# Gated spectral filter and token MLP: the order of the last two additions, and the last token block in two column halves

## The chip, the cores and the metric

The kernel runs on one core of a Trainium2 chip. The metric is the device time of one execution in microseconds; a profiled execution also gives a trace of every engine. TensorE (PE) multiplies matrices into PSUM, ScalarE (ACT) and VectorE (DVE) read PSUM and write SBUF, GpSimd (POOL) works on SBUF, and SyncE (SP) issues all transfers.

## The reference

Two branches work on the same input `x` of 2048 tokens by 512 channels, in bf16, and are blended per token by a sigmoid gate. Branch A is a two-dimensional FFT, a product with complex weights, and the inverse FFT. Branch B is a layernorm followed by an MLP over the token axis (2048 to 1792 to 2048).

```python
def _A_ref(x, w_r, w_i):
    X = rfft2(x.astype(float32), axes=(-2, -1))
    X = X * (w_r + 1j * w_i)
    return irfft2(X, s=(S, D)).astype(bfloat16)

def _B_ref(x, w1, b1, w2, b2):
    h = _layernorm(x, axis=-1)
    u = gelu(einsum("bsd,sf->bdf", h, w1) + b1)
    y = einsum("bdf,fs->bds", u, w2) + b2
    return y.transpose(0, 2, 1)

g = sigmoid((x * gate_w).sum(-1, keepdims=True))
return g * a + (1 - g) * b
```

## The kernel before

Tokens lie on the 128 partitions in 16 blocks: block `r` holds one token for each partition and all 512 channels, a tile of 128x512. `x` and `hn` in SBUF hold the 16 blocks of the input and of its layernorm. `tb` is another name for `x`: the result of block `r` is written over the input block `r`, which nobody reads any more by then. In the same way `z3` is another name for `hn`.

Branch B runs in two products. The first multiplies `hn` by the weights `w1` and goes through GELU on ScalarE (line 478) into `gl`, 14 tiles of 128x512. The second product (line 749) makes block `r` out of 14 matmuls, one for each tile of `gl`, that accumulate in one PSUM bank. Its weights for block `r`, 448 KB, are loaded ahead into a slot of the SBUF tiles `w1a` or `w1b` (line 746), whose first contents are used up by then; blocks 14 and 15 use slots 8 and 9 of `w1a` again.

Branch A is a chain of short matrix products with evictions, two round trips through DRAM and an elementwise product between them. It ends in a transform of each block: one matmul with the 128x128 matrix `t1i` and the block `z3[r]` (line 759).

The two branches meet at the end. The gate `g` becomes three tables with one column per block: `omg` is 1 - g, `omb` is (1 - g) times the bias b2, and `gs` is g times the scale of the inverse FFT; POOL makes them out of a tanh on ScalarE (lines 736 to 740). For each block:

- ScalarE evicts the second product with its scale and bias: `tb[r] = omg * product + omb`, bf16 (line 752, named `ye`).
- VectorE adds the transform from PSUM: `tb[r] = gs * transform + tb[r]` (line 762, named `fin`).
- SP sends `tb[r]` to DRAM, 128 KB (line 765, named `out`).

PSUM has eight banks. Four are handed out in pairs (the pool `pair`: the transforms of two blocks share one), and four singly (the pool `fb`: one for each second product).

The order on every engine is written out by a planner, the class `Plan` (lines 39 to 165). Each operation is added with an engine, an estimated cost in ns, a priority (a lower one goes first), and keys that it reads and writes. The planner repeats one step: of all operations whose inputs and buffers are known, it takes the one that can start earliest by the estimates, and among equals the one with the lower priority, and then the one added first. That fixes each engine's order; the engines then run in this order and wait for each other by semaphores. So the place in the program text decides only between equals. Priorities that matter here: `T1i` (transform) 60 + r, second product 300 + r, load of its weights 62 + 3.05 r, outputs 200.

Of the kernel before, what the change touches and what calls it, by code (L numbers as in the profile page):

```python
# [8 lines left out]
ActF = mybir.ActivationFunctionType  # L9
# [6 lines left out]
D = 512  # L16
NR = 16
NG = 16
NQ = 4
NPAIR = 2  # L20
F = 1792
NFT = 14
# [16 lines left out]
class Plan:  # L39
# [13 lines left out]
    def add(self, eng, cost, emit, prio, r=(), w=(), name="", nbytes=0, h=(), acq=(), t0=0.0):  # L53
        op = Op()
        op.eng, op.cost, op.emit, op.prio, op.name, op.bytes = eng, cost, emit, prio, name, nbytes
        op.deps, op.succ, op.ready, op.end, op.start = set(), [], t0, None, None
        op.seq = len(self.ops)
        op.acq = tuple(acq)
        op.holds = tuple(set(h) | set(acq))
        for x in op.holds:  # L60
            x.left += 1
            if x in op.acq:
                x.by = op
            else:
                op.deps.add(x.by)
        for k in r:
            if k in self.last_write:
                op.deps.add(self.last_write[k])
            self.readers.setdefault(k, []).append(op)
        for k in w:  # L70
            if k in self.last_write:
                op.deps.add(self.last_write[k])
            for o in self.readers.get(k, ()):
                op.deps.add(o)
            self.last_write[k] = op
            self.readers[k] = []
        op.deps.discard(op)
        self.ops.append(op)
        return op
# [89 lines left out]
def kernel(  # L169
# [17 lines left out]
    add = pl.add  # L187
    V, A, G, T, Q = nc.vector, nc.scalar, nc.gpsimd, nc.tensor, nc.sync
# [4 lines left out]
    x = sb([P, NR, D], "x")  # L193
    hn = sb([P, NR, D], "hn")
    gl = sb([P, NFT, D], "gl")
# [32 lines left out]
    omg = sb([P, NR], "omg", F32)  # L228
    gs = sb([P, NR], "gs", F32)
    omb = sb([P, NR], "omb", F32)  # L230
# [3 lines left out]
    ps = psp.tile([P, 8, 512], F32, name="ps")  # L234
# [3 lines left out]
    tb = x  # L238
# [8 lines left out]
    for b in range(0, NR, 2):  # L247
        k = b // 2
# [63 lines left out]
    mul, plus, band, shr = Alu.mult, Alu.add, Alu.bitwise_and, Alu.arith_shift_right  # L312
# [12 lines left out]
    for k, (n, sh, m) in enumerate(BITS):  # L325
        add("DVE", 75, lambda k=k, sh=sh, m=m: V.tensor_scalar(ci[:, k:k + 1], pcol, sh, m, op0=shr, op1=band), -94,
            r=["pcol"], w=[("ci", k)], name=n)
    add("DVE", 90, lambda: V.tensor_copy(cf[:, 0:len(BITS)], ci[:]), -93, r=[("ci", k) for k in range(len(BITS))],
        w=[("c", n) for n in col], name="cf")
# [63 lines left out]
    for j in range(4):  # L393
        for cc in range(2):
            add("ACT", 600, lambda j=j, cc=cc: A.activation(t2v[:, :, cc, :, j], svv[:, cc], ActF.Copy,  # L395
                                                            scale=f(f"d{j}")), 1.5, r=["sv", ("c", f"d{j}")] + TMPK, w=["t2"])
# [30 lines left out]
    for k, (o, s, key) in enumerate(((768.0, ecol[:, 0:1], "ecol"), (768.0, ecol[:, 1:2], "ecol"),  # L427
# [11 lines left out]
        r=["rrow", ("c", "ck")] + TMPK, w=["rg"])  # L439
# [9 lines left out]
        r=["sv2"] + [("c", f"d{j}") for j in range(4)] + TMPK, w=["t2i"], name="exp", t0=28000.0)  # L449
# [14 lines left out]
    for b in range(NR):  # L464
        add("DVE", 605, lambda b=b: V.bn_stats(out=stats[:, b, :], in_=x[:, b, :]), b, r=[("x", b)],  # L465
            w=[("stats", b)], name="bn")
        add("DVE", 90, lambda b=b: V.bn_aggr(out=mv[:, b, :], in_=stats[:, b, :]), b - 0.5, r=[("stats", b)],  # L467
            w=[("mv", b)], name="aggr")
        add("DVE", 62, lambda b=b: V.tensor_single_scalar(mv[:, b, 1:2], mv[:, b, 1:2], 1e-5, op=plus), b - 0.6,
            w=[("mv", b)], name="eps")  # L470
# [3 lines left out]
                                                    op0=Alu.subtract, op1=mul), b - 10,  # L474
            r=[("x", b), ("mv", b), ("rstd", b)], w=[("hn", b)], name="hn")
# [10 lines left out]
    for b in range(NR):  # L486
        for ft in range(FT1):
# [3 lines left out]
                stop=(b == NR - 1)), 100 + b if b < 13 else 113 + 0.1 * ft,  # L491
                r=[("w1a", b), ("hn", b)] + [("over", b, j) for j in range(b * 768 // 2048, ((b + 1) * 768 - 1) // 2048 + 1)],
                w=[("acc", ft)],
                name="p1", h=[hold], acq=[hold] if b == 0 and first else [])
# [12 lines left out]
    for k in range(NFT - FT1):  # L507
        ft = FT1 + k
        w, wk, wl = wslot(k)
        load(w, w1bh[k].rearrange("a r f -> a (r f)"), 26 + 3.45 * k, wl, 524288)  # L510
        wv = w.rearrange("p (r f) -> p r f", f=P)
        hb = Hold("fb")
# [8 lines left out]
    for r2 in range(8):  # L521
        hs = Hold("sth")
        for k in range(2):
            r = 2 * r2 + k
            add("PE", 216, lambda r=r, k=k: T.matmul(ps[:, k], lhsT=t1[:], rhs=x[:, r, :], start=True,  # L525
                                                     stop=True), 10 + r, r=["t1", ("x", r)],
                w=[("psT", k)], name="T1", h=[ht], acq=[ht] if r == 0 else [])
            add("ACT", 480, lambda hs=hs, k=k: A.copy(st4[:, hs.idx, k], ps[:, k]), 0,  # L528
                r=[("psT", k)], w=[("st1", r2)], name="T1e", h=[ht], acq=[hs] if k == 0 else [])
        add("SP", 440, lambda r2=r2, hs=hs: Q.dma_start(out=scr1[2 * r2:2 * r2 + 2].rearrange("r p d -> p r d"),  # L530
                                                        in_=st4[:, hs.idx]), 5.5, r=[("st1", r2)],
            w=[("scr1", r2)], nbytes=262144, name="w1", h=[hs])
    s1v = scr1[:].rearrange("r (c g) d -> (r c) g d", g=NG)
    zh = [Hold("zz", q) for q in range(NQ)]
    for q in range(NQ):
        add("SP", 440, lambda q=q: Q.dma_start(out=z2[:, 4 * q:4 * q + 4], in_=s1v[:, 4 * q:4 * q + 4]), 6 + 0.1 * q,
            r=[("scr1", k) for k in range(8)], w=[("z2", q)], nbytes=524288, name="r1", h=[zh[q]], acq=[zh[q]])

    def pslot(hold, k):
        return ps[:, 2 * hold.idx + k]  # L540
# [7 lines left out]
    for q in range(NQ):  # L548
# [3 lines left out]
        for h in range(2):  # L552
            hp = Hold("pair")
            for k in range(2):
                g = 4 * q + 2 * h + k
                for s in range(4):
                    add("PE", 56, lambda g=g, s=s, k=k, hp=hp: T.matmul(  # L557
                        pslot(hp, k)[:, s * P:(s + 1) * P], lhsT=z2[:, g, s * P:(s + 1) * P],
                        rhs=t2[:, g].rearrange("p k c l i -> p (k c l i)"), start=True, stop=True),
                        20 + q, r=["t2", ("z2", q)], w=[kq("pT2", h, k, s)], name="T2", h=[hp, zh[q]],  # L560
                        acq=[hp] if k == 0 and s == 0 else [])
# [3 lines left out]
                r=[kq("pT2", h, k, s) for k in range(2) for s in range(4)], w=[kq("t2o", h)], name="T2e",  # L565
                h=[hp, ht2], acq=[ht2] if h == 0 else [])
# [6 lines left out]
        def fold2(V_op, sl, ht2=ht2, hpm=hpm, hfo=hfo):  # L573
# [4 lines left out]
            acq=[hpm])  # L578
# [3 lines left out]
            name="f2", h=[hpm], acq=[hfo])  # L582
        add("DVE", 605, lambda f=fold2: f(V.tensor_sub, slice(1, 3)), 50, r=pmk, w=[kq("fo", 1), kq("fo", 2)],
            name="f2", h=[hpm, hfo])
        for t in range(2):
            hp = Hold("pair")
            for e in range(2):
# [3 lines left out]
                    r=["td", kq("fo", cl)], w=[kq("pD", cl)], name="D", h=[hp, hfo], acq=[hp] if e == 0 else [])  # L591
            add("ACT", 905, lambda t=t, hp=hp, huv=huv: A.copy(uv[:, huv.idx, t], pview(hp)), 2.5,  # L592
                r=[kq("pD", 2 * t), kq("pD", 2 * t + 1)], w=[kq("uv", t)], name="De", h=[hp, huv],
                acq=[huv] if t == 0 else [])
# [15 lines left out]
        def Yv(hy=hy):  # L610
# [5 lines left out]
            h=[huv], acq=[hx])  # L616
        add("DVE", 605, lambda U=U, W_=W_, X=X: V.tensor_sub(X()[:, :, 2:0:-1], U(), W_()), pw, r=uk, w=xk, name="w",
            h=[huv, hx])
        for s in range(2):
            def wv_(m, s=s):  # L620
# [3 lines left out]
                r=xk + [("wq", q)], w=tk, name="w", h=[hx, htb], acq=[htb] if s == 0 else [])  # L624
            add("DVE", 605, lambda X=X, m=wr, wv_=wv_, ss_=ss_: V.tensor_mul(X()[:, :, ss_], X()[:, :, ss_], wv_(m)), pw,
                r=[("wq", q)], w=xk, name="w", h=[hx])
        add("DVE", 605, lambda X=X: V.tensor_sub(X()[:, :, 0:4:3], X()[:, :, 0:4:3], tbw[:, :, 1:3]), pw, r=tk, w=xk,
            name="w", h=[hx, htb])
        add("DVE", 605, lambda X=X: V.tensor_add(X()[:, :, 1:3], X()[:, :, 1:3], tbw[:, :, 0:4:3]), pw, r=tk, w=xk,
            name="w", h=[hx, htb])  # L630
        add("DVE", 605, lambda X=X, Yv=Yv: V.tensor_add(Yv()[:, 0], X()[:, :, 0:2], X()[:, :, 2:4]), pw, r=xk, w=yk,
            name="w", h=[hx], acq=[hy])
        add("DVE", 605, lambda X=X, Yv=Yv: V.tensor_sub(Yv()[:, 1], X()[:, :, 3::-3], X()[:, :, 1:3]), pw, r=xk, w=yk,
            name="w", h=[hx, hy])
        if q == 0:
# [3 lines left out]
            for k, (t, c_) in enumerate(((0, 0), (1, 1), (1, 0), (0, 1))):  # L639
                add("POOL", 400, lambda k=k, t=t, c_=c_: G.tensor_tensor(spt[:, k], sUV(t), w0[c_], op=mul), 0,  # L640
                    r=uk + [("wq", 0)], w=["spt"], h=[huv])
            add("POOL", 400, lambda: G.tensor_tensor(spc[:, 0], spt[:, 0], spt[:, 1], op=plus), 0, r=["spt"], w=["spc"])
            add("POOL", 400, lambda: G.tensor_tensor(spc[:, 1], spt[:, 2], spt[:, 3], op=Alu.subtract), 0, r=["spt"],
                w=["spc"])
            for t in range(2):
                add("DVE", 90, lambda t=t, Y=Y: V.tensor_copy(
                    Y()[:, t].rearrange("p e n (c k) -> p e n c k", c=2)[:, :, 0, :, 0], spc[:, t]), 59, r=["spc"],
                    w=yk, h=[hy])
# [3 lines left out]
                r=["lw"], w=["li"])  # L652
            ts("POOL", 250, lr[:], lr[:], 0.5, None, mul, None, 0, [], ["lr"])
            ts("POOL", 250, li[:], li[:], 0.5, None, mul, None, 0, [], ["li"])
        for t in range(2):
            add("SP", 440, lambda q=q, t=t, huv=huv: Q.dma_start(
                out=lf[16 * t:16 * t + 16, q].rearrange("p c k -> p (c k)"),
                in_=uv[0:1, huv.idx, t, 0].rearrange("o (n c) -> o n c", c=32)), 5, r=[kq("uv", t)],
                w=[kq("lf", t)], nbytes=20000, name="lane", h=[huv])
        lk = [kq("lf", 0), kq("lf", 1)]  # L660
        add("POOL", 400, lambda q=q: G.tensor_tensor(lt[:, 0], lf[:, q], lr[:, q], op=mul), 0, r=lk + ["lr"],
            w=["lt"])
# [3 lines left out]
            r=["lt"], w=[kq("lo")])  # L666
        add("POOL", 400, lambda q=q: G.tensor_tensor(lo[:, q, 1], lt[:, 0, 1], lt[:, 1, 0], op=plus), 0,
            r=["lt"], w=[kq("lo")])
        for t in range(2):
            add("SP", 440, lambda Y=Y, q=q, t=t: Q.dma_start(  # L670
                out=Y()[0:1, t, 0], in_=lo[16 * t:16 * t + 16, q].rearrange("p c k -> p (c k)")), 4,
                r=[kq("lo")] + yk, w=[kq("yl", t)], nbytes=20000, name="lane", h=[hy])
# [6 lines left out]
        for h in range(2):  # L679
            hp = Hold("pair")  # L680
            first = True
            for cl, (t, e) in ((1, (0, 1)), (3, (1, 1)), (0, (0, 0)), (2, (1, 0))):
                for k in range(2):
# [3 lines left out]
                        lhsT=Y()[:, t, e, n:n + 4].rearrange("p n c -> p (n c)"),  # L687
                        rhs=tdi[:, cl], start=True, stop=True), 40 + q,
                        r=["tdi"] + yk + ([kq("yl", t)] if e == 0 else []), w=[kq("pI", h, k, cl)],
                        name="Di", h=[hp, hy], acq=[hp] if first else [])  # L690
# [49 lines left out]
    add("POOL", 200, lambda: G.tensor_tensor(omb[:], omg[:], smf[:, 14:30], op=mul), 0, r=["omg", "smf"], w=["omb"])  # L740

    slots = [8, 9, 10, 11, 12, 13, 0, 1, 2, 3, 4, 5, 6, 7, 8, 9]
    for r in range(NR):
        w, wk, wl = wslot(slots[r])
        wv = w[:, 0:NFT * P].rearrange("p (t a) -> p t a", a=P)
        load(wv, w2h[r], 62 + 3.05 * r, wl, 458752)
        hb = Hold("fb")
        for ft in range(NFT):
            add("PE", 216, lambda ft=ft, wv=wv, hb=hb: T.matmul(  # L749
                ps[:, 2 * NPAIR + hb.idx], lhsT=wv[:, ft], rhs=gl[:, ft, :], start=(ft == 0), stop=(ft == NFT - 1)),  # L750
                300 + r, r=wk + [("gl", ft)], w=[("y", r)], name="p2", h=[hb], acq=[hb] if ft == 0 else [])
        add("ACT", 665, lambda r=r, hb=hb: A.activation(tb[:, r, :], ps[:, 2 * NPAIR + hb.idx], ActF.Identity,  # L752
                                                        bias=omb[:, r:r + 1], scale=omg[:, r:r + 1]), 2.2,
            r=[("y", r), "omb", "omg"], w=[("x", r)], name="ye", h=[hb])
    for r2 in range(NR // 2):
        hp = Hold("pair")
        for k in range(2):
            r = 2 * r2 + k
            add("PE", 216, lambda r=r, hp=hp, k=k: T.matmul(pslot(hp, k), lhsT=t1i[:], rhs=z3[:, r, :], start=True,  # L759
                                                            stop=True), 60 + r, r=["t1i", ("hn", r)],  # L760
                w=[("pL", r)], name="T1i", h=[hp], acq=[hp] if k == 0 else [])
            add("DVE", 660, lambda r=r, hp=hp, k=k: V.scalar_tensor_tensor(  # L762
                tb[:, r, :], pslot(hp, k), gs[:, r:r + 1], tb[:, r, :], op0=mul, op1=plus), 30,
                r=[("pL", r), "gs"], w=[("x", r)], name="fin", h=[hp])
            add("SP", 440, lambda r=r: Q.dma_start(out=out[r], in_=tb[:, r, :]), 200, r=[("x", r)], w=[("out", r)],
                nbytes=131072, name="out")
    pl.run()
    global _PLAN
    _PLAN = pl
# [69 lines left out]
```

## Time and profile before

| | |
|---|---|
| Median of 6 runs | 135.73 us |
| Lowest and highest of the 6 | 133.41 and 137.38 us |
| Profiled execution, its own time | 133.49 us |
| Its span, first to last instruction | 131.7 us |
| Mean granted TensorE clock | 0.994 |
| TensorE busy | 123.5 us (94%) in 648 matmuls |
| VectorE, ScalarE, POOL busy | 93.8, 71.4, 41.0 us |
| Second product: matmuls, booked length of one | 224, 379 ns |
| Last step on ScalarE (line 752), mean of one | 782 ns, 16 times |
| Last step on VectorE (line 762), mean of one | 746 ns, 16 times |
| Output of a block, issue to landing | 1.7 us (median), 16 times |

The profiled execution took 2.2 us less than the median of the other runs; the runs themselves are 4 us apart. Busy time of TensorE counts the booked length of each matmul, from its start to the end of its passage through the array; matmuls overlap, so the distance between two starts tells what one costs in a stream. "Issue to landing" of a transfer runs from the instruction on SP to the arrival of its last bytes.

### The profile page before, as it was taken

To read this page: it belongs to the slowest core of one execution; us is meant where nothing else is said; L and a number is where in the kernel's file an instruction comes from. 1 tells how busy PE (TensorE), PEld (TensorE's weight loads), DVE (VectorE), ACT (ScalarE), POOL (GpSimd) and SP (SyncE) were. 2 spreads that over 40 slices of the span, in tenths; PEclk is the share of its full clock that TensorE was granted. 3 is DMA by queue.
4 is the path that set the end of the run, shared out by engine and by line. 5 is a ranking of instruction groups with operands and counts; after the bars stand their busy time and mean duration, and the time that the engine had idled before them with its cause. 6 is when DMAs were issued, how large, how long until landed. Compare 5 with 4: busy or idle time off the path is not lost.

```text
span 131.7 us, 1982 instructions
## 1 busy us (share of the span) xinstructions
PE 123.5 (94%) x648; PEld 58.0 (44%) x648; DVE 93.8 (71%) x245; ACT 71.4 (54%) x98; POOL 41.0 (31%) x87
## 2 busy tenths in 40 slices
PE   6979999999799999999989999999999999999960
PEld 2223444443565444445445454544444444444420
DVE  7999899889799979999999998803400089322221
ACT  5378899169685784763254668539572222113320
POOL 5299964970440049997270000000000000000000
PEclk9999999999999999999999999999999999999997
DMA  4999989998989899999995327210323985411111
GB/s 119 266 331 386 339 185 388 353 373 294 346 281 348 299 335 314 291 340 329 344 380 168 135 43 260 96 69 0 159 98 130 362 285 200 163 41 40 40 40 40
DMA packets 15962, 29.67 MB, mean 225 GB/s; under 512 B 1968, under 2 KB 10320, under 8 KB 15952
## 3 DMA queue, kind: packets, MB, share of 16 engines
q1 hardware_dynamic: 15952, 29.55, 65.6%
q8 instruction: 5, 0.08, 0.2%
q14 instruction: 5, 0.04, 0.1%
HBM read 23.23 MB, written 6.29 MB: 224 GB/s over the span
## 4 chain that ended last, share of the span: by engine, by line
PE 71%; DMA 17%; ACT 5%; SPq 2%; issue 1%; DVE 1%
PE ps L749 37%; PE ps L514 16%; DMA x<-in_x_dram 5%; DMA scr_104<-st 4%; DMA z_66<-scr_104 4%; PE ps L489 4%; DMA yw<-lo 4%; PE ps L557 3%; PE ps L685 3%; PE ps L759 3%; PE ps L718 3%; PE ps L589 3%; SPq L245 2%; ACT st L528 2%; ACT t_76 L395 2%; PE ps L525 1%
## 5 line engine op out<-in xcount | busy, mean ns | idle before, releaser
L514 PE MATMUL ps<-hn,w1b 128*128 128x512 bf16 x128 | 30.7, 379 | 0.0
L762 DVE SCALAR_TENSOR_TENSOR x<-ps,gs,x 128x512 bf16<-128x512 f32 x16 | 11.1, 746 | 24.0 <-PE ps L759 12.1
L752 ACT ACTIVATE x<-ps,omb,omg 128x512 bf16<-128x512 f32 x16 | 12.5, 782 | 27.3 <-PE ps L749 27.3
L749 PE MATMUL ps<-gl,w1a 128*128 128x512 bf16 x112 | 26.6, 379 | 0.0
L749 PE MATMUL ps<-gl,w1b 128*128 128x512 bf16 x112 | 25.6, 379 | 0.0
L489 PE MATMUL ps<-hn,w1a 128*128 128x512 bf16 x96 | 22.8, 379 | 0.0
L514 PEld LDWEIGHTS <-w1b 128*128 128x128 bf16 x128 | 12.1, 98 | 12.7
L749 PEld LDWEIGHTS <-w1b 128*128 128x128 bf16 x112 | 11.0, 98 | 13.2
L749 PEld LDWEIGHTS <-w1a 128*128 128x128 bf16 x112 | 10.7, 98 | 11.4
L478 ACT ACTIVATE gl<-ps,smf 128x512 bf16<-128x512 f32 x14 | 9.1, 693 | 9.9 <-PE ps L514 9.0
L489 PEld LDWEIGHTS <-w1a 128*128 128x128 bf16 x96 | 9.4, 98 | 11.1 <-issue 0.2
L528 ACT CAST st<-ps 128x512 bf16<-128x512 f32 x16 | 9.2, 608 | 4.4 <-PE ps L525 3.4
L471 POOL TENSOR_TENSOR rstd<-mv,cst 128x1 f32<-128x1 f32 x16 | 9.9, 633 | 5.4 <-DVE mv L467 3.2
L733 DVE CUSTOM_DVE_ANT_0 junk<-x,gwb 128x512 bf16<-128x512 bf16 x16 | 11.2, 697 | 0.2
L465 DVE BATCH_NORM_STATS2 stats<-x 128x6 f32<-128x512 bf16 x16 | 10.6, 670 | 0.0
L692 ACT CAST z_66<-ps 128x1024 bf16<-128x1024 f32 x8 | 7.7, 1014 | 4.8 <-PE ps L685 4.8
L699 DVE TENSOR_TENSOR big<-z_66 128x1024 bf16<-128x1024 bf16 x8 | 5.4, 685 | 6.6 <-ACT z_66 L692 6.6
L592 ACT CAST uv<-ps 128x1024 bf16<-128x1024 f32 x8 | 7.9, 1017 | 2.4 <-DMA lf<-uv 1.9
L722 ACT CAST st<-ps 128x1024 bf16<-128x1024 f32 x8 | 7.8, 1018 | 2.5 <-PE ps L718 2.3
L562 ACT CAST big<-ps 128x1024 bf16<-128x1024 f32 x8 | 7.8, 1013 | 1.2 <-PE ps L557 1.1
L525 PE MATMUL ps<-x,t_80 128*128 128x512 bf16 x16 | 6.7, 439 | 1.3 <-DMA x<-in_x_dram 1.1
L473 DVE TENSOR_SCALAR hn<-x,mv,rstd 128x512 bf16<-128x512 bf16 x16 | 6.7, 432 | 0.6 <-POOL rstd L471 0.5
(100 smaller groups left out, 152.4 us busy)
## 6 DMA issues: line engine op xcount, KB each, us to landing
w1b<-in_w1b_dram SPq DMA_DIRECT2D x8, 512.0 KB, 5.2
w1a<-in_w_dram SPq DMA_DIRECT2D x8, 448.0 KB, 4.9
w1b<-in_w_dram SPq DMA_DIRECT2D x8, 448.0 KB, 5.0
w1a<-in_w1a_dram SPq DMA_DIRECT2D x8, 384.0 KB, 6.2
x<-in_x_dram SPq DMA_DIRECT2D x8, 256.0 KB, 5.8
scr_104<-st SPq DMA_DIRECT2D x8, 256.0 KB, 5.8
z_66<-scr_104 SPq DMA_DIRECT2D x4, 512.0 KB, 6.9
wq<-in_wf_dram SPq DMA_DIRECT2D x4, 512.0 KB, 5.0
```

What stands on the lines that cost most here:

```text
L465: add("DVE", 605, lambda b=b: V.bn_stats(out=stats[:, b, :], in_=x[:, b, :]), b, r=[("x", b)], w=[("stats", b)], name="bn")
L471: add("POOL", 530, lambda b=b: G.tensor_tensor(rstd[:, b:b + 1], mv[:, b, 1:2], cst[:, 1:2], op=Alu.pow), b - 200, r=[("mv", b), "cst"], w ...
L478: add("ACT", 572, lambda: A.activation(gl[:, ft, :], ps[:, bank()], ActF.Gelu_apprx_tanh, bias=smf[:, ft:ft + 1], scale=1.0), prio, r=r + ...
L489: add("PE", 216, lambda b=b, ft=ft, bank=bank: T.matmul(ps[:, bank()], lhsT=w1a[:, b, ft * P:(ft + 1) * P], rhs=hn[:, b, :], start=(b == 0 ...
L514: add("PE", 216, lambda b=b, wv=wv, hb=hb: T.matmul(ps[:, 2 * NPAIR + hb.idx], lhsT=wv[:, b], rhs=hn[:, b, :], start=(b == 0), stop=(b == ...
L525: add("PE", 216, lambda r=r, k=k: T.matmul(ps[:, k], lhsT=t1[:], rhs=x[:, r, :], start=True, stop=True), 10 + r, r=["t1", ("x", r)], w=[(" ...
L528: add("ACT", 480, lambda hs=hs, k=k: A.copy(st4[:, hs.idx, k], ps[:, k]), 0, r=[("psT", k)], w=[("st1", r2)], name="T1e", h=[ht], acq=[hs] ...
L592: add("ACT", 905, lambda t=t, hp=hp, huv=huv: A.copy(uv[:, huv.idx, t], pview(hp)), 2.5, r=[kq("pD", 2 * t), kq("pD", 2 * t + 1)], w=[kq(" ...
L733: add("DVE", 735, lambda b=b: V.tensor_tensor_reduce(junk[:], x[:, b, :], gwb[:], 1.0, 0.0, mul, plus, accum_out=glog[:, b:b + 1]), 61.5, ...
L749: add("PE", 216, lambda ft=ft, wv=wv, hb=hb: T.matmul(ps[:, 2 * NPAIR + hb.idx], lhsT=wv[:, ft], rhs=gl[:, ft, :], start=(ft == 0), stop=( ...
L752: add("ACT", 665, lambda r=r, hb=hb: A.activation(tb[:, r, :], ps[:, 2 * NPAIR + hb.idx], ActF.Identity, bias=omb[:, r:r + 1], scale=omg[: ...
L762: add("DVE", 660, lambda r=r, hp=hp, k=k: V.scalar_tensor_tensor(tb[:, r, :], pslot(hp, k), gs[:, r:r + 1], tb[:, r, :], op0=mul, op1=plus ...
```

## The change

For the last two blocks, 14 and 15, the two additions swap their order. ScalarE first evicts the transform with its gate and the bias: `tb[r] = gs * transform + omb` (named `ab`). VectorE then adds the second product straight from PSUM: `tb[r] = omg * product + tb[r]` (named `fin`). For blocks 0 to 13 nothing is changed.

The second product of block 15 is cut into two halves of 256 columns, each with its own PSUM bank, its own 14 matmuls, its own `fin` and its own output of 64 KB. The loop over the second product becomes a function `second(r)`; it is called for blocks 0 to 13 where the loop stood, and for 14 and 15 behind the transforms, since `fin` reads what `ab` writes. The cost given to the planner for a half is 108 instead of 216 ns for a matmul and 390 instead of 660 ns for `fin`.

```diff
     slots = [8, 9, 10, 11, 12, 13, 0, 1, 2, 3, 4, 5, 6, 7, 8, 9]
-    for r in range(NR):
+    def second(r):
         w, wk, wl = wslot(slots[r])
         wv = w[:, 0:NFT * P].rearrange("p (t a) -> p t a", a=P)
         load(wv, w2h[r], 62 + 3.05 * r, wl, 458752)
-        hb = Hold("fb")
-        for ft in range(NFT):
-            add("PE", 216, lambda ft=ft, wv=wv, hb=hb: T.matmul(
-                ps[:, 2 * NPAIR + hb.idx], lhsT=wv[:, ft], rhs=gl[:, ft, :], start=(ft == 0), stop=(ft == NFT - 1)),
-                300 + r, r=wk + [("gl", ft)], w=[("y", r)], name="p2", h=[hb], acq=[hb] if ft == 0 else [])
-        add("ACT", 665, lambda r=r, hb=hb: A.activation(tb[:, r, :], ps[:, 2 * NPAIR + hb.idx], ActF.Identity,
-                                                        bias=omb[:, r:r + 1], scale=omg[:, r:r + 1]), 2.2,
-            r=[("y", r), "omb", "omg"], w=[("x", r)], name="ye", h=[hb])
+        for c in range(2 if r == NR - 1 else 1):
+            cs = slice(256 * c, 256 * c + 256) if r == NR - 1 else slice(0, D)
+            hb = Hold("fb")
+            for ft in range(NFT):
+                add("PE", 216 if r < NR - 1 else 108, lambda ft=ft, wv=wv, hb=hb, cs=cs: T.matmul(
+                    ps[:, 2 * NPAIR + hb.idx, cs], lhsT=wv[:, ft], rhs=gl[:, ft, cs], start=(ft == 0),
+                    stop=(ft == NFT - 1)), 300 + r, r=wk + [("gl", ft)], w=[("y", r, c)], name="p2", h=[hb],
+                    acq=[hb] if ft == 0 else [])
+            if r < NR - 2:
+                add("ACT", 665, lambda r=r, hb=hb: A.activation(tb[:, r, :], ps[:, 2 * NPAIR + hb.idx], ActF.Identity,
+                                                                bias=omb[:, r:r + 1], scale=omg[:, r:r + 1]), 2.2,
+                    r=[("y", r, c), "omb", "omg"], w=[("x", r)], name="ye", h=[hb])
+            else:
+                add("DVE", 660 if r < NR - 1 else 390, lambda r=r, hb=hb, cs=cs: V.scalar_tensor_tensor(
+                    tb[:, r, cs], ps[:, 2 * NPAIR + hb.idx, cs], omg[:, r:r + 1], tb[:, r, cs], op0=mul, op1=plus), 30,
+                    r=[("y", r, c), "omg", ("ab", r)], w=[("x", r, c)], name="fin", h=[hb])
+                add("SP", 440, lambda r=r, cs=cs: Q.dma_start(out=out[r][:, cs], in_=tb[:, r, cs]), 200, r=[("x", r, c)],
+                    w=[("out", r, c)], nbytes=131072 if r < NR - 1 else 65536, name="out")
+
+    for r in range(NR - 2):
+        second(r)
     for r2 in range(NR // 2):
         hp = Hold("pair")
         for k in range(2):
...
+            if r >= NR - 2:
+                add("ACT", 665, lambda r=r, hp=hp, k=k: A.activation(tb[:, r, :], pslot(hp, k), ActF.Identity,
+                                                                     bias=omb[:, r:r + 1], scale=gs[:, r:r + 1]), 2.2,
+                    r=[("pL", r), "omb", "gs"], w=[("x", r), ("ab", r)], name="ab", h=[hp])
+                continue
...
+    for r in range(NR - 2, NR):
+        second(r)
     pl.run()
```

## The prediction

> **What bounds the kernel now.** I read four views in this order: the page's clock and engine rows, the chain that ended last, its tail in order of time, and the timeline of the last microseconds. The page first:
>
> ```profile
> PE   6979999999799999999989999999999999999960
> ...
> DVE  7999899889799979999999998803400089322221
> ACT  5378899169685784763254668539572222113320
> POOL 5299964970440049997270000000000000000000
> PEclk9999999999999999999999999999999999999997
> DMA  4999989998989899999995327210323985411111
> ```
>
> Each digit is a fortieth of the span, 3.3 us. In the second half TensorE is full while VectorE and ScalarE fall to 2 or 3 tenths, POOL has nothing from slice 24 on, and the DMA engines stand at a tenth in the last five slices. So near the end only two things can cost time: TensorE's own work, and what must follow its last matmul. The chain in order of time, from 117 us:
>
> ```profile
> 117.44 9.94 PE ps L749 x46
> 127.38 0.03 issue
> 127.41 0.79 ACT x L752
> 128.19 0.03 issue
> 128.22 0.75 DVE x L762
> ```
>
> The 46 second-product matmuls run without a hole (9.94/46 = 0.216 us each), then come two evictions in series: ScalarE's scale and bias, VectorE's gated sum. That is 128.22 + 0.75 - 127.38 = 1.59 us after TensorE stops. The timeline adds the rest:
>
> ```profile
> 116.84 0.59 PE L759 MATMUL ps<-hn,t1i 128*128 128x512 bf16 x2
> ...
> 118.34 0.78 ACT L752 ACTIVATE x<-ps,omb,omg 128x512 bf16<-128x512 f32 x1 [2.67 <-PE ps L749]
> ...
> 124.38 0.78 ACT L752 ACTIVATE x<-ps,omb,omg 128x512 bf16<-128x512 f32 x1 [2.24 <-PE ps L749]
> ...
> 127.41 0.78 ACT L752 ACTIVATE x<-ps,omb,omg 128x512 bf16<-128x512 f32 x1 [2.24 <-PE ps L749]
> 128.22 0.75 DVE L762 SCALAR_TENSOR_TENSOR x<-ps,gs,x 128x512 bf16<-128x512 f32 x1 [2.27 <-ACT x L752]
> 129.00 0.33 SPq L765 DMA_DIRECT2D out_dram<-x  x1
> ```
>
> The transforms of blocks 14 and 15 are in PSUM at about 117.4, ten microseconds before they are used. The last output is issued at 129.00; outputs take 1.7 us to land (fastest and median, 2.9 the slowest), and the span closes at 131.7.
>
> **The change part by part.** The sum is made against the profiled execution: 133.49 us, of which 131.7 is span and 1.8 lies around it. The median of the runs is 135.73, 2.2 us more, and I carry the difference over unchanged.
>
> *Removed.* For block 15, the ScalarE step between last matmul and last sum leaves the end: 0.79 plus one 0.03 handover, 0.82 us. For block 14 the same step leaves too, but TensorE works on for 3 us behind it, so it is worth nothing.
>
> *Halved.* The last sum covers 256 columns. No row shows this on PSUM. The full one takes 743 ns. [...] The upper end is the one row of this operation with 256 columns:
>
> ```profile
> L438 DVE SCALAR_TENSOR_TENSOR yw<-yw,cf 128x256 f32<-128x256 f32 x1 | 0.5, 528 | 0.0
> ```
>
> It is all f32 and from SBUF, so I take 490 from 392 to 528, near the PSUM row less its columns. [...] New tail: 0.03 + 0.49 = 0.52 instead of 1.59, a gain of 1.07 us (1.17 at the best end, 1.03 at the worst).
>
> *Added on TensorE.* Block 15 becomes 28 matmuls of 256 columns and 28 weight loads instead of 14 and 14. No row has 256 columns; two rows lie on either side. 512 columns step by 216 ns. Of 128 columns, in the timeline:
>
> ```profile
> 84.66 0.61 PE L685 MATMUL ps<-tdi,yw 128*128 128x128 bf16 x8
> ```
>
> and, for all 64 of the line, shortest, median and longest in ns:
>
> ```profile
> L685 PE MATMUL ps<-tdi,yw x64: 219/219/230, 61.8 to 88.9; 128*128 128x128 bf16 x64
> ```
>
> Eight of them, each with its own weights, span 0.61 us, and the last is booked at 0.219, so they step by (0.61 - 0.219)/7 = 56 ns. A weight load booked at 98 ns therefore doesn't set the pace even at a quarter of the width. A line through 56 and 216 gives 109 at 256: 28 x 0.109 = 3.05 against 14 x 0.216 = 3.02, a loss of 0.03. [...] The row is this kernel's own, with weights changed at every matmul, so I use 0.03, with 0 and 0.7 as ends.
>
> *Added on ScalarE.* Two evictions (gated transform plus bias) of the form of L752, 0.78 each, start when the transforms end, about 117.25. ScalarE idles 2.67 us before 118.34, so the first is free; the second ends near 118.8 and holds block 12's eviction, queued behind it, back by 0.5 us. Waiting for that are block 12's sum on VectorE and its PSUM bank. VectorE is idle 2.7 us around it, and block 14's product, the earliest that can want the bank, starts at 121.2, 1.6 us after the late eviction ends. Cost nothing; with that cover gone, the 0.5. `omb` and `gs` come from POOL, which has been idle since slice 24.
>
> *Moved on VectorE.* Block 14's sum now waits for its product: 124.4 to 125.15. The first half of block 15 is done by TensorE about 125.87, so its sum runs 125.9 to 126.4 on an idle VectorE. The second half needs a free bank at 125.87; should it be given block 14's, that was read out 0.7 us before.
>
> *DMAs.* The w2 loads of blocks 14 and 15 stand later in the text, but their due times are unchanged, and the last load from w2 starts at 77.5, 44 us before block 14 begins. SP issues one output more, 0.33 us, at about 126.4, and is free at 126.8, before it is wanted at 127.9. The last output carries 64 KB, still in 128 rows. The DMA share 0.09 over the last 4.2 us is 0.38 us of work for 128 KB; if bytes count, half is saved, if packets count, nothing. I take 0.1 of 0 to 0.19. A loss would need a slower landing, 2.9 instead of 1.7; that belongs to outputs in the crowded slices and I see no cause here. The close after landing stays.
>
> Sum: -1.07 + 0.03 - 0.1 = -1.14 us. Profiled execution 133.49 to 132.35; median 135.73 to **134.6 us**, 0.8% less.
>
> **The rivals.**
>
> *A wait takes the step's place.* If the second half's sum is made to wait for the first half's output (same tile row, neighbouring columns), it starts when that lands: issued 126.4, plus 1.7 is 128.1, sum to 128.6, output issued 128.65 instead of 129.00. Gain 0.35 + 0.1: median 135.3. Against it: eleven sums write rows of the same tile from 105.92 within 7.34 us, 0.67 apart, while outputs of other rows of it are in flight, so waits go by region. For it: no row shows two column halves. Chance 0.10.
>
> *TensorE pays for the halves: slower.* The place is block 15's product, the price 28 steps; above (3.02 + 1.14 - 0.03)/28 = 147 ns a step the change loses. At its limit, where a 256-column matmul takes a 512-column one's 216 ns, the product costs 6.05 us, 3.0 more: profiled 135.35, median 137.6. [...] Chance 0.08, with most of it short of the limit.
>
> *It does not do what it says.* The planner orders by readiness, then priority. Were the two transforms placed late, the new ScalarE steps would stand at the end again and the median stay at 135.7. But their priorities are 74 and 75 against 300 and more for the products, and the trace has them at 116.84. Chance 0.02.
>
> *More than the tail.* If the packed last output closes faster, or the order after 117 us happens to sit better, another 0.5 to 1.5 us could come: 133.3. Nothing shows it: TensorE is full until 127.4. Chance 0.05.
>
> **How the numbers follow.** The main case has the remaining 0.75. Its own span is narrow (-0.3 to -1.4 us by the ends above), but the six runs shown lie between 133.41 and 137.38, and a change within 2% is about what a measurement of this kernel can't tell from none. Two of the six lie at 133.41; moved by -1.14 they are at 132.3. Faster by over 2% means below 133.0: that needs most of the new runs in this low group: four or more of six come to one chance in ten if the group holds a third of all runs, and to 0.34 if it holds half; two runs of six don't tell these apart, and I take 0.22. So faster: 0.75 x 0.22 plus 0.05 for more than the tail and a little of the first rival, 0.23. Slower by over 2% means over 138.4: the TensorE case at its limit with an unlucky median, 0.03, and a stall that no row shows, 0.04: 0.07. Within: 0.70. The range runs from 132.2 (main case, low group) to 136.6 (TensorE half-way to its limit, 136.1, or the main case among the high runs, 137.38 - 1.14 = 136.2).
>
> **What would show it.** Right: no ScalarE step behind the last matmul; a sum of 128x256 of about 490 ns as the last work; two ScalarE steps near 117.3; 28 matmuls with 109 ns between starts; last output issued near 127.95 and the span near 130.6. Wrong: a hole in TensorE between 121 and 127.5, steps above 120 ns, the last sum released by an output transfer instead of TensorE, or any other order ahead of 116 us.

## The result and the profile after

| | before | changed |
|---|---|---|
| Median of all runs (20 and 10) | 134.47 us | 133.1 us |
| Lowest and highest | 132.95, 137.98 | 131.57, 136.66 |
| Ratio of times, with 95% interval | 1 | 0.9866 (0.9817 to 0.9914) |
| Profiled execution | 133.49 us | 132.02 us |
| Its span | 131.72 us | 130.25 us |

The ratio is taken over the undisturbed runs of both kernels, the medians over all, so the two need not agree to the last tenth. The change makes the kernel faster by 0.9 to 1.8%, which is within 2%. Measured again with more runs (below) the ratio was 0.991 (0.9857 to 0.9963).

The page of the changed kernel, busy tenths by slices of 3.3 us:

```profile
PE   6959999999999999999997999999999999999990
...
DVE  7999899969999989999999996901600059622231
ACT  5368999167984795653253686728772220235200
...
DMA  4999989999889988999986229030124996610211
```

ScalarE's last two slices read 0 and 0, where they read 2 and 0. TensorE is as full as before up to its end. The chain in order of time, start and length in us:

```profile
117.10 9.98 PE ps L751 x60
127.08 0.03 issue
127.10 0.48 DVE x L760
```

The second product now counts 60 matmuls, 32 whole and 28 halves, and takes 9.98 us instead of 9.94. Behind it stands one step of 0.48 us instead of two of 0.79 and 0.75. The timeline of the last stretch:

```profile
116.50 0.59 PE L772 MATMUL ps<-hn,t1i 128*128 128x512 bf16 x2
...
116.92 1.45 ACT L776 ACTIVATE x<-ps,omb,gs 128x512 bf16<-128x512 f32 x2 [1.60 <-PE ps L772]
...
118.26 0.78 ACT L756 ACTIVATE x<-ps,omb,omg 128x512 bf16<-128x512 f32 x1
...
124.04 0.75 DVE L760 SCALAR_TENSOR_TENSOR x<-ps,omg,x 128x512 bf16<-128x512 f32 x1 [1.46 <-PE ps L751]
124.82 3.12 SPq L763 DMA_DIRECT2D out_dram<-x  x3
125.57 0.48 DVE L760 SCALAR_TENSOR_TENSOR x<-ps,omg,x 128x256 bf16<-128x256 f32 x1 [0.78 <-PE ps L751]
127.10 0.48 DVE L760 SCALAR_TENSOR_TENSOR x<-ps,omg,x 128x256 bf16<-128x256 f32 x1 [1.04 <-PE ps L751]
```

The two new ScalarE steps run at 116.92, ten microseconds ahead of the end. Block 12's eviction follows at 118.26, without idle time before it: it had to wait. All three new sums are released by TensorE, none by a transfer. The last output is issued at 124.82 + 3.12 - 0.33 = 127.61.

**A measure that does not depend on what lies ahead.** The spans differ by 1.47 us, but block 14's product, the first with weights from `w1a` again, started at 121.16 before and at 120.82 now. That 0.34 us is not the change's: on every engine the two programs give the same instructions in the same order up to the start of block 14's product, apart from the new ScalarE steps. From there to the end of the span, before and now (start, end and length in us, then busy time and count of each engine, clock, DMA share and GB/s):

```profile
121.16:131.72 10.56, 6.21 (x29) 2.64 (x27) 2.25 (x3) 2.33 (x3) 0.00 (x0) 0.92 0.11 38
```

```profile
120.82:130.25 9.44, 6.24 (x43) 4.00 (x41) 2.47 (x4) 0.78 (x1) 0.00 (x0) 0.94 0.16 51
```

I call this the last stretch; it is used for all experiments, as the difference of its two ends (here 10.56 and 9.43). The expectations below were written with spans read to a tenth of a microsecond (131.7, 130.3), so their stretches are up to 0.05 us off: their 10.54 is 10.56 here, their 9.48 is 9.43, their 3.22 us after TensorE are 3.17, and the gain between the two traces is 1.13 us, not 1.06.

| kernel | from block 14's start to TensorE's end | after it | last stretch |
|---|---|---|---|
| before | 6.22 | 4.34 | 10.56 |
| changed | 6.26 | 3.17 | 9.43 |
| changed, repeated | 6.26 | 3.17 | 9.43 |
| swap alone | 6.22 | 3.58 | 9.80 |
| swap alone, repeated | 6.23 | 3.59 | 9.82 |
| halves alone | 6.26 | 3.76 | 10.02 |
| swap of block 15 only | 6.25 | 3.18 | 9.43 |
| one output for block 15 | 6.25 | 3.37 | 9.62 |
| quarters | 6.32 | 2.81 | 9.13 |
| 384 and 128 columns | 6.26 | 2.97 | 9.23 |
| 384 and 128, repeated | 6.25 | 2.96 | 9.21 |
| all blocks in halves | 6.29 | 3.17 | 9.46 |
| transforms late | | | 11.69 |
| 256, 192 and 64 columns | | | 9.26 |

"TensorE's end" is where the last step behind TensorE is released: the last sum, or where the order is the old one the last eviction. The three pairs of traces of one kernel agree within 0.02 us.

### The profile page after: what moved, and what is told of

Its sections match the earlier page's. It is cut to its first block, busy times and chain, and to the rows that moved or that the text cites. A ratio compares the mean times of both kernels' runs of the same rounds, so it can differ in the third digit from the quotient of the medians.

```text
span 130.3 us, 2013 instructions
## 1 busy us (share of the span) xinstructions
PE 122.9 (94%) x662; PEld 59.5 (46%) x662; DVE 94.1 (72%) x246; ACT 71.2 (55%) x98; POOL 40.5 (31%) x87
## 3 DMA queue, kind: packets, MB, share of 16 engines
HBM read 23.23 MB, written 6.29 MB: 227 GB/s over the span
## 4 chain that ended last, share of the span: by engine, by line
PE 56%; DVE 20%; DMA 9%; POOL 8%; issue 2%; ACT 2%; SPq 1%
PE ps L751 36%; PE ps L514 7%; DMA x<-in_x_dram 5%; DMA yw<-lo 5%; POOL rstd L471 3%; DVE stats L465 3%; PE ps L557 3%; PE ps L718 3%; PE ps L772 3%; DVE hn L473 2%; PE ps L489 2%; POOL t_76 L308 2%; PE ps L685 2%; DVE tbw L623 2%; DVE xw L615 2%
## 5 line engine op out<-in xcount | busy, mean ns | idle before, releaser
L751 PE MATMUL ps<-gl,w1a 128*128 128x512 bf16 (+1 forms) x126 | 26.7, 355 | 0.0
L780 DVE SCALAR_TENSOR_TENSOR x<-ps,gs,x 128x512 bf16<-128x512 f32 x14 | 9.6, 745 | 19.5 <-PE ps L772 12.1
L756 ACT ACTIVATE x<-ps,omb,omg 128x512 bf16<-128x512 f32 x14 | 10.9, 781 | 19.9 <-PE ps L751 19.9
L751 PEld LDWEIGHTS <-w1a 128*128 128x128 bf16 x126 | 12.0, 98 | 10.3
L489 PEld LDWEIGHTS <-w1a 128*128 128x128 bf16 x96 | 9.4, 98 | 11.9 <-issue 0.9
L471 POOL TENSOR_TENSOR rstd<-mv,cst 128x1 f32<-128x1 f32 x16 | 9.1, 577 | 6.5 <-DVE mv L467 4.2
```

Source lines behind the costliest of these rows:

```text
L471: add("POOL", 530, lambda b=b: G.tensor_tensor(rstd[:, b:b + 1], mv[:, b, 1:2], cst[:, 1:2], op=Alu.pow), b - 200, r=[("mv", b), "cst"], w ...
L489: add("PE", 216, lambda b=b, ft=ft, bank=bank: T.matmul(ps[:, bank()], lhsT=w1a[:, b, ft * P:(ft + 1) * P], rhs=hn[:, b, :], start=(b == 0 ...
L751: add("PE", 216 if r < NR - 1 else 108, lambda ft=ft, wv=wv, hb=hb, cs=cs: T.matmul(ps[:, 2 * NPAIR + hb.idx, cs], lhsT=wv[:, ft], rhs=gl[ ...
```

## The experiments

The edits are shown in excerpts; the costs and sizes given to the planner follow the new pieces in each.

**The swap alone.** Block 15 in one piece, additions in the new order for 14 and 15.

```diff
-        for c in range(2 if r == NR - 1 else 1):
-            cs = slice(256 * c, 256 * c + 256) if r == NR - 1 else slice(0, D)
+        for c in range(1):
+            cs = slice(0, D)
```

> The swap alone, block 15 in one piece. Theory A (the time after the last matmul is the sum of the steps left there): from the end of TensorE to the end of the span 0.03 + 0.75 + 2.73 = 3.5 us, where the kernel before has 4.32 and the changed one 3.22; time about 0.8 us under before. Rival B (the gain comes from the halves, the swap only moves work): no more than 0.3 us under before.

The chain in order of time:

```profile
116.54 9.94 PE ps L751 x46
126.49 0.02 issue
126.51 0.75 DVE x L760
```

TensorE's 9.94 us are those of the kernel before, and 3.58 us follow it (130.07 - 126.49), 0.76 less than before. Theory A had 3.5; the last output landed later than it took (2.81 us after the last sum). The swap brings two thirds of the gain, and by the trace rival B falls. The four runs, from 131.85 to 135.21 us, gave no ratio. Repeated with more runs:

> The swap alone, once more. Theory A: the stretch from block 14's start to the end 9.8 us as before (0.7 under the kernel before), ratio near 0.994.

The last stretch was 9.82 us; the ratio was 0.9906 (0.9858 to 0.9955), which holds the expected 0.994 but is also that of the whole change. The times alone don't tell the two kernels apart.

**The halves alone.** The additions in the old order, the eviction and the sum of block 15 in halves.

```diff
+        for c in range(2 if r == NR - 1 else 1):
+            cs = slice(256 * c, 256 * c + 256) if r == NR - 1 else slice(0, D)
...
-        add("ACT", 665, lambda r=r, hb=hb: A.activation(tb[:, r, :], ...
+            add("ACT", 665 if r < NR - 1 else 420, lambda r=r, hb=hb, cs=cs: A.activation(tb[:, r, cs], ...
```

> The halves alone, additions in the old order. Theory A: a ScalarE step of 256 columns, estimated 0.58 us (0.78 less the 0.2 us by which the casts of 1024 and 512 columns differ per 256), then a sum of 0.48: tail 0.03 + 0.58 + 0.03 + 0.48 + 2.72 = 3.84 us, 0.48 under before. Rival B: the tail is near the 3.22 of the changed kernel, and the time 1.1 us or more under before.

The same view:

```profile
117.34 9.98 PE ps L751 x60
127.32 0.03 issue
127.34 0.57 ACT x L755
127.92 0.02 issue
127.94 0.48 DVE x L767
```

Both steps are shorter, but they still stand in series: 3.76 us after TensorE, where 3.84 was expected, and a ratio of 0.995 (0.9893 to 1.0007). The two parts overlap in what they save: about 0.75 and 0.54 us alone, 1.13 together, since the swap takes away the eviction that the halves only shorten (from 0.78 to 0.57).

**Block 14 left in the old order.**

```diff
-            if r < NR - 2:
+            if r < NR - 1:
...
-    for r in range(NR - 2):
+    for r in range(NR - 1):
...
-            if r >= NR - 2:
+            if r >= NR - 1:
...
-    for r in range(NR - 2, NR):
+    for r in range(NR - 1, NR):
```

> Halves and swap for block 15, block 14 left in the old order. Theory A: block 14's eviction was 3 us ahead of the end in any case, so the tail stays 3.2 us and the time is that of the changed kernel. Rival C (block 14's swap helps, by a bank or an output that is free earlier): a hole in TensorE before the second half, or a tail over 3.4 us.

```profile
120.31 9.98 PE ps L751 x60
130.28 0.03 issue
130.31 0.48 DVE x L760
```

TensorE runs through, 3.18 us follow it, and the last stretch is the changed kernel's. Block 14's part of the change is worth nothing at the end; rival C falls. The time, 0.9835 (0.9758 to 0.9912) of before, is not told apart from the changed kernel's.

**One output for block 15.** Two halves, but a single transfer of 128 KB after the second sum.

```diff
-                add("SP", 440, lambda r=r, cs=cs: Q.dma_start(out=out[r][:, cs], in_=tb[:, r, cs]), 200, ...
+                if r == NR - 2 or c == 1:
+                    add("SP", 440, lambda r=r: Q.dma_start(out=out[r], in_=tb[:, r, :]), 200, ...
```

> Both halves of block 15 go out in one transfer of 128 KB after the second sum. Theory A: the landing is mostly a fixed time; tail 3.2 to 3.3 us, 0 to 0.1 over the changed kernel. Rival D (the smaller last output is a real part of the gain): 0.19 us or more over the changed kernel.

The wait of SP for its last output, in us in total, times, longest; first this kernel, then the changed one:

```profile
SPq L853 <- DMA out_dram<-x: 1.4, 1, 1.4
```

```profile
SPq L852 <- DMA out_dram<-x: 1.2, 1, 1.2
```

The last stretch is 0.19 us longer than the changed kernel's: what rival D expected, and about twice the most that theory A allowed. Of this, 0.04 us is that SP issues the output 0.07 us behind the sum instead of 0.03. Over the traces with halves or one piece and early transforms the time from the end of the last sum to the end of the span is 2.75, 2.81, 2.82 and 2.86 us with a last output of 128 KB (before, swap alone twice, this one), and 2.66 or 2.67 us in all five with one of 64 KB. So the smaller output is a real part of the gain: 0.08 us from the kernel before to the changed one, 0.14 to 0.19 against the other three. Why the kernel before landed sooner than those three is not known. The ratio to before was 0.9885 (0.9801 to 0.997), too wide to show it.

**Quarters.** Block 15 in four pieces of 128 columns.

```diff
-        for c in range(2 if r == NR - 1 else 1):
-            cs = slice(256 * c, 256 * c + 256) if r == NR - 1 else slice(0, D)
+        for c in range(4 if r == NR - 1 else 1):
+            cs = slice(128 * c, 128 * c + 128) if r == NR - 1 else slice(0, D)
```

> Block 15 in four column quarters of 128, each with its own bank, sum and output of 32 KB. Theory A: a sum of 128 columns is 0.48 less 128/0.96 ns = 0.34 us, so 0.14 us less tail; block 15's product 56 x 0.056 = 3.14 us instead of 3.05, 0.09 more; the landing 1.6 us or a little less: within 0.1 us of the changed kernel. Rival E (outputs with rows of 256 bytes land later): the last wait for an output 0.3 us or more longer, slower than the changed kernel. Rival F (the quarters wait for banks): a hole in TensorE before the fourth quarter.

From the groups of the last 11 us by shape, and the list of transfers with size and median us to landing:

```profile
L751 PE MATMUL ps<-gl,w1a 128*128 128x128 bf16 x56 | 3.3, 219 | 0.0
...
L760 DVE SCALAR_TENSOR_TENSOR x<-ps,omg,x 128x128 bf16<-128x128 f32 x4 | 1.4, 351 | 1.3 <-PE ps L751 1.3
```

```profile
out_dram<-x SPq DMA_DIRECT2D x15, 128.0 KB, 1.7
out_dram<-x SPq DMA_DIRECT2D x4, 32.0 KB, 1.4
```

The sum took 351 ns instead of 340, and the product 0.06 us more than with halves. The expectation's 1/0.96 ns a column is the step between the changed kernel's sums of 512 and 256 columns, (751 - 484)/256 = 1.04. What I had too small was the gain by the output: rows of 256 bytes land 0.3 us sooner than a whole block, not later, and 2.43 us follow the last sum (2.67 with halves). The last stretch is 0.30 us shorter than the changed kernel's instead of about the same; rivals E and F fall. The time, 0.9947 (0.9878 to 1.0017) of before, doesn't show it.

**384 and 128 columns.**

```diff
-            cs = slice(256 * c, 256 * c + 256) if r == NR - 1 else slice(0, D)
+            cs = (slice(0, 384), slice(384, 512))[c] if r == NR - 1 else slice(0, D)
```

> Block 15 in two uneven pieces, 384 and 128 columns. Theory A: tail 0.14 us shorter than with halves (3.08 against 3.22), product the same 3.07 us. Two things could take it back: the first piece's sum (about 0.61 us) ends 0.2 us ahead of the second's matmuls, so none is expected from VectorE; rows of 256 bytes in the last output would show as a longer landing.

```profile
127.49 0.62 DVE L760 SCALAR_TENSOR_TENSOR x<-ps,omg,x 128x384 bf16<-128x384 f32 x1 [1.52 <-PE ps L751]
128.27 0.35 DVE L760 SCALAR_TENSOR_TENSOR x<-ps,omg,x 128x128 bf16<-128x128 f32 x1 [0.16 <-PE ps L751]
```

VectorE is free 0.16 us before the last piece arrives, so this is near the most uneven cut into two that it can follow. 2.97 us follow TensorE, 0.20 less than with halves where 0.14 was expected: 0.13 by the sum, 0.07 by the smaller last output (2.60 us after the sum instead of 2.67). The quarters, which end on a piece of the same size, have a last stretch 0.1 us shorter still, though their product takes longer: the span closed 2.43 us after their last sum. Their last output was issued 0.78 us behind another of 32 KB, here it is 0.48 us behind one of 96 KB; whether that is the reason was not tried. Repeated next to the changed kernel:

> Block 15 in 384 and 128 columns, once more, on the same chip as the changed kernel. Theory A (its stretch from block 14's start to the end was 9.21 us against 9.48 with halves and 10.54 before): 0.27 us under the changed kernel, ratio to before near 0.990. Rival I (times are set ahead of that stretch): any ratio, with the stretch 9.2 us again.

> The changed kernel once more, with more rounds. Theory A (all of the gain lies behind block 14's start, 1.06 us in the two traces): ratio to before near 0.992. Rival I (something ahead of it gained as well, as the first ratio of 0.9866 would have it, 1.8 us): near 0.987, and block 14's product starting earlier than in other traces.

The stretches came out again: 9.21 us here and 9.43 for the changed kernel. The ratios to before were 0.991 (0.9867 to 0.9953) and 0.991 (0.9857 to 0.9963); the first measurement of 384 and 128 had given 0.9989 (0.9938 to 1.004). So the uneven cut is 0.2 us better in the traces, and not shown to be better in the times. Two measurements of one kernel lie 0.8% apart here, as much as the whole gain, so the intervals don't hold all of the scatter between measurements. The changed kernel's second ratio fits theory A's 0.992 but holds rival I's 0.987 too; the first, 0.9866, does not quite hold 0.992 (its interval ends at 0.9914). No row points to a gain ahead of the last stretch: the order of instructions up to it is the same, and in the repeated trace block 14's product started late, at 124.50. Whether the times gained more than the 1.13 us of the stretch stays open.

**All blocks in halves.** 210 more matmuls and weight loads; each bank of blocks 0 to 14 is filled in two column halves.

```diff
+            hs_ = [cs] if r == NR - 1 else [slice(0, 256), slice(256, 512)]
+            for i, sl in enumerate(hs_):
+                for ft in range(NFT):
+                    add("PE", 108, lambda ft=ft, wv=wv, hb=hb, sl=sl: T.matmul(
+                        ps[:, 2 * NPAIR + hb.idx, sl], lhsT=wv[:, ft], rhs=gl[:, ft, sl], start=(ft == 0),
...
```

> The second product of all 16 blocks in column halves (same bank for blocks 0 to 14, all sums and outputs as in the changed kernel): 210 more matmuls and weight loads. Theory A (256 columns step by 109 ns): 15 x 14 x (2 x 0.109 - 0.216) = 0.4 us over the changed kernel. [...]

```profile
118.52 10.06 PE ps L753 x92
128.58 0.03 issue
128.60 0.48 DVE x L762
```

The 92 halves are the work of the changed kernel's 60 matmuls and take 0.08 us more; 32 of them were split, so a split costs 2.5 ns, and a half steps by 10.06/92 = 109 ns. For 210 splits that makes an estimate of 0.5 us, near theory A's 0.4. The ratio to before is 0.9973 (0.9904 to 1.0042), 0.8 or 1.4 us above the changed kernel's two ratios; with intervals of this width it neither bears out the 0.5 us nor excludes it.

**The transforms late.** The transforms of blocks 14 and 15 behind all products.

```diff
-                                                            stop=True), 60 + r, r=["t1i", ("hn", r)],
+                                                            stop=True), 60 + r if r < NR - 2 else 400 + r, r=["t1i", ("hn", r)],
```

> The transforms of blocks 14 and 15 get the priority 400 + r, so that they come behind all second products. Theory A (the swap is worth something only because the transform is ready early): after the last product 2 transforms (0.43 us), two ScalarE steps and a sum stand at the end: tail about 2 us longer than in the changed kernel, so slower than before by about 0.9 us. Rival H (the swap helps by using fewer ScalarE steps late): no slower than before.

```profile
129.10 0.59 PE L772 MATMUL ps<-hn,t1i 128*128 128x512 bf16 x2
129.52 1.45 ACT L776 ACTIVATE x<-ps,omb,gs 128x512 bf16<-128x512 f32 x2 [5.52 <-PE ps L772]
130.33 1.54 DVE L760 SCALAR_TENSOR_TENSOR x<-ps,omg,x 128x512 bf16<-128x512 f32 x3 [5.54 <-ACT x L776]
131.11 1.30 SPq L763 DMA_DIRECT2D out_dram<-x  x3
```

Everything that the change had moved ahead stands at the end again. The last stretch is 134.72 - 123.03 = 11.69 us, 2.26 more than in the changed kernel and 1.13 more than before; theory A had about 2 and 0.9. The ratio to before, 1.014 (0.993 to 1.0351), points the same way without settling it. The swap is worth something because the transform is ready early; rival H has nothing for it.

**256, 192 and 64 columns.**

```diff
+        for c in range(3 if r == NR - 1 else 1):
+            cs = (slice(0, 256), slice(256, 448), slice(448, 512))[c] if r == NR - 1 else slice(0, D)
```

> Block 15 in three pieces of 256, 192 and 64 columns. Theory A: the last sum, of 64 columns, takes 0.35 less 64/0.96 ns = 0.28 us, the product 14 x (0.109 + 0.083 + about 0.030) = 3.1 us: the stretch from block 14's start to the end 9.1 to 9.25 us, against 9.21 with 384 and 128. Rival J (64 columns are too few for TensorE: each still costs 56 ns for its weight load): 0.36 us longer. Rival K (three outputs close together hold up the last one on SP, 0.33 us each): the last issue more than 0.1 us behind the last sum.

```profile
128.66 0.54 PE L751 MATMUL ps<-gl,w1a 128*128 128x64 bf16 x13
...
128.83 0.69 DVE L760 SCALAR_TENSOR_TENSOR x<-ps,omg,x 128x192 bf16<-128x192 f32 x2 [0.67 <-PE ps L751]
129.28 0.33 SPq L763 DMA_DIRECT2D out_dram<-x  x1
```

The last two outputs together, and the shortest, median and longest of the four issues in ns:

```profile
129.28 0.81 SPq L763 DMA_DIRECT2D out_dram<-x  x2
```

```profile
L763 SPq DMA_DIRECT2D out_dram<-x x4: 332/332/382, 126.9 to 129.7; - x4
```

The 64-column matmuls step by (0.54 - 0.193)/12 = 29 ns (one is booked at 193), so rival J falls. But the last stretch is 132.19 - 122.93 = 9.26 us, just above the expected 9.1 to 9.25 and no better than two pieces. The last sum runs directly behind the one of 192 columns and ends at 128.83 + 0.69 = 129.52; its output is issued at 129.28 + 0.81 - 0.38 = 129.71, 0.43 after the one before and about 0.18 after its sum. No view shows two outputs issued closer together than this (other transfers of SP follow each other at 0.37, in the kernel before at 28.01 and 28.38, so what sets the 0.43 is open); in the 384 and 128 kernel they are 0.48 apart, and there the sum is ready just in time. Rival K was right, though not by 0.33 us each. The ratio, 0.9827 (0.9745 to 0.9909) from six runs, is the lowest of all, but the last stretch does not bear it out.

## Why the prediction was right

Predicted were 134.6 us from a median of 135.73, -1.14 us or 0.8%. The last stretch fell by 1.13 us in both traces of the changed kernel; the measured ratios are 0.9866 and 0.991. That the median came out at 133.1 and not at 134.6 says little of the change: with 20 runs instead of six the median of the kernel before is itself 134.47. The mechanism was the one forecast. By its steps:

- *Removed.* The 0.82 us of eviction and handover are gone. The swap alone shows 0.76 by the last stretch; the other 0.06 is its landing, 2.81 us after the last sum where the kernel before had 2.75.
- *Halved.* 490 ns were taken, from 392 to 528, and 484 measured. No row of the kernel before shows 490, and no run shows the 392, on which the best end of 1.17 us rests; only 528 was a row's. What the runs show instead are the groups by shape of the kernel with three pieces, the one with 384 and 128 columns, and the changed one:

```profile
L760 DVE SCALAR_TENSOR_TENSOR x<-ps,omg,x 128x64 bf16<-128x64 f32 x1 | 0.3, 283 | 0.0
```

```profile
L760 DVE SCALAR_TENSOR_TENSOR x<-ps,omg,x 128x384 bf16<-128x384 f32 x1 | 0.6, 618 | 1.5 <-PE ps L751 1.5
```

```profile
L760 DVE SCALAR_TENSOR_TENSOR x<-ps,omg,x 128x256 bf16<-128x256 f32 x2 | 1.0, 484 | 1.8 <-PE ps L751 1.8
L760 DVE SCALAR_TENSOR_TENSOR x<-ps,omg,x 128x512 bf16<-128x512 f32 x1 | 0.8, 751 | 1.5 <-PE ps L751 1.5
```

  The slope is (751 - 283)/448 = 1.04 ns a column, and 216 ns are fixed; the whole sum's 751 ns less 256 columns at this slope are the 484. Two halves cost 968 ns instead of 751; it doesn't count, since the first one's sum, 125.57 to 126.05, runs under TensorE, which works until 127.08.
- *Added on TensorE.* 0.03 us were taken, 0.04 measured, a step of 109 ns; the line through the rows of 128 and 512 columns held: the steps are 29, 56 and 109 ns at 64, 128 and 256 columns, with a weight load each time. No run shows the 0.7 us that the prediction took as its upper end; the most was 0.10, with quarters (6.32 us where the kernel before has 6.22).
- *Added on ScalarE.* The transform's start to block 12's eviction was 1.50 us before (116.84 to 118.34) and is 1.76 now, a delay of 0.26 where 0.5 was predicted: two steps of 0.78 booked take 1.45 together. Nothing at the end is later for it.
- *DMAs.* 0.1 us was taken from 0 to 0.19. Between the two profiles it is 0.08; the run with one output puts it at up to 0.19.
- *The rivals.* No sum waited for a transfer; TensorE did not pay for the halves; the planner put the transforms where it had them, and the run that put them late shows what that would have cost. More than the tail is suggested by the first ratio, 1.8 us; no trace shows it, and the second ratio neither confirms it nor rules it out. One sum of the prediction is off without effect: the step at which TensorE's halves would eat the gain is (3.02 + 1.14 + 0.03)/28 = 150 ns, not 147, since the 1.14 already has the 0.03 taken off.

The profiled execution fell by 1.47 us where 1.14 was predicted. Of this 1.13 us lie in the last stretch and 0.34 arose before block 14's start, in work that the change does not touch.

## What to carry to other kernels

At the end of a kernel, list what stands between the last result of the bounding engine and the last transfer; a term that is ready early should be combined first, so that only one operation is left for the late one. Then make the last piece small: here 128 of 512 columns saved 0.2 us more than halves behind one piece of 384, and 0.3 us more behind three of 128. A last piece of 64 behind one of 192 saved less, since VectorE and SP were not yet done with the piece ahead of it. Where runs are 4 us apart, compare such changes by a stretch of the trace that starts behind the noise, and read its ends to the hundredth: rounding to a tenth had hidden 0.07 us of the gain here.

## What was not expected of the hardware

**Small outputs land sooner.** The medians to landing were 1.7 us for 128 KB, 1.6 for 96, 1.5 to 1.6 for 64, 1.4 to 1.5 for 32 (rows of 256 bytes), and 1.5 for 16 KB (rows of 128 bytes). So 1.5 of 1.7 us are left at an eighth of the bytes, and rows of 128 bytes land no later than rows of 1024.

**The spread of the runs arises far ahead of the change.** Block 14's product started anywhere between 120.3 and 122.5 us in eight traces that share the order up to there, and at 122.93, 124.48 and 124.50 in three more (256, 192 and 64 columns, and the repeated swap alone and changed kernel). Waits of TensorE in the swap alone, the halves alone (same chip, started at 120.27 and 121.06) and the quarters (another chip, 122.52), in us in total, times, longest:

```profile
PE ps L525 <- DMA x<-in_x_dram: 0.8, 2, 0.5
...
PE ps L557 <- DMA z<-scr: 0.2, 1, 0.2
```

```profile
PE ps L525 <- DMA x<-in_x_dram: 1.2, 3, 0.8
PE ps L685 <- DMA yw<-lo: 0.9, 1, 0.9
...
PE ps L557 <- DMA z<-scr: 0.2, 1, 0.2
```

```profile
PE ps L557 <- DMA z<-scr: 1.4, 1, 1.4
PE ps L525 <- DMA x<-in_x_dram: 1.4, 2, 0.9
...
PE ps L685 <- DMA yw<-lo: 1.1, 1, 1.1
```

The late ones waited longer for the input (`x`) and for transfers of 1 KB into `yw`, the quarters also for the round trip of the forward transform (`z`). In stretches of 10 us the DMA share of the three traces was 0.80 to 1.02 up to 70 us, and 0.34 to 0.44 in the next one, in which the quarters' wait for `yw` ended (at 72.41). All waits of TensorE in this view add up to 3.2, 4.0 and 5.8 us: 0.8 and 2.6 more, for starts 0.8 and 2.3 us later. Over the eight traces it is a tendency and no more: the kernel before started at 121.16 with 3.8 us of waits, the one with one output at 120.86 with 4.5. Behind block 14's start nothing of the spread is left, since the last stretch repeats within 0.02 us. What sets these waits was not tried.
